# In the first expert layer a piece's second product runs three steps behind its first instead of two, with a third buffer for the high part

## The chip, the cores and the metric

The kernel runs on one NeuronCore of a Trainium2 chip. The metric is the device time of one execution in microseconds (us), median of three runs. Five engines work at once, each through its own queue in order: TensorE (PE, matrix products into PSUM), VectorE (DVE), ScalarE (ACT), GpSimd (POOL), and SyncE (SP), which here issues nearly all DMAs. PEld is TensorE's loading of weights, which overlaps the products.

## The reference, cut to what matters

```python
attn_out = _attn_ref(...)                 # linear attention, 8 x 8 heads, 576 tokens
x = attn_out ... reshape(B * S, H * D)    # 4608 tokens x 512
# first expert layer
h = x @ w_in                              # 512 -> 2048
g = h - np.tanh(h)
x = (g @ w_out).astype(np.float32)        # 2048 -> 512
# second expert layer
a = x @ w1
b = x @ w2
h = a * b @ w3
return (h @ w_out).astype(np.float32)
```

## The kernel before

Three stages follow one another: `attention()`, `moe1()` (the first expert layer) and `moe2()` (the second). Every fp32 operand of a large product is split into a high and a low part, so that one product is three TensorE products (high x high, low x high, high x low) summed in PSUM. In the names, `wih` and `wil` are the high and low part of a weight, `gh` and `gl` those of g.

**The first expert layer.** The 4608 tokens are 9 blocks of 512 (`NB`), the 2048 hidden columns 16 chunks of 128 (`NFC`). Step n = 16 j + i handles chunk i of block j, so there are 144 steps, numbered from 0. A step has two products on TensorE, of 12 matmuls of 128x512 each. The first, `mm1(n)` (L444, its matmuls are L456, tile `h`), gives a 128x512 tile of h. The second, `mm2` (L518, matmuls L527, tile `y`), multiplies g by 128 rows of `w_out` and adds into four banks y0 to y3 (`ps_y`, one buffer each), which gather a block over its 16 steps. Between the two lies `act_g(n)` (L470), which makes g = h - tanh(h), with a polynomial where h is small. It is a chain over three engines:

- ACT: u = h squared (L480), t = tanh h (L481), s (L482);
- DVE: p from h and u (L486), t = h - t (L488), p from s and p (L490), a mask into u (L492), a copy under that mask into t (L494);
- ACT: `gh`, the high part of t (L498); POOL: `gl` = t - `gh` (L499).

**What sets the order.** The schedule is by hand: every engine runs its instructions in the order in which the program writes them. The loop over n (L580) writes `mm1(n)`, then `mm2(n - LAG)` with `LAG = 2`, then `act_g(n)`. So TensorE's queue reads `mm1(n)`, `mm2(n-2)`, `mm1(n+1)`, `mm2(n-1)` and so on. Tiles `gh` and `gl` have two buffers each (`p3`), h three (`ps_h`).

**The end of a block.** Where `mm2` finishes a block, it hands the four y banks to the `act_g` of the same loop pass, as `ys`. There `y_out` (L504) copies them to SBUF: y0 to y2 on ACT behind s (L513), y3 on DVE behind the masked copy L494 (L515), and SP stores them (L516). The next block's first `mm2` writes the same banks, so it waits for these copies. With `LAG = 2` the block that ends at step 16j - 1 is copied in `act_g(16j + 1)`, and `mm2(16j)` comes in the pass behind.

**Work in between.** Into `act_g` and behind it the loop puts single operations on other things (`some()`, up to six): the conversion of 64-bit weights to high and low parts (`conv_steps`, L84: absolute value `et` on ACT L94, a maximum and a shift on DVE L98 and L101, a merge L104 on DVE, an integer part `ec` on ACT L109, an add on POOL L112, high part `wh` on ACT L116, low part `wl` on POOL L119), from step 0 to 13 for late chunks and from 16 to about 128 for the second layer's weights. Every third of the first twelve steps of a block ends with the split of a part of the next block's x (`split_x`: `xh` on ACT L747, `xl` on POOL L748).

**The seam to the second layer.** For n from 144 on, `mm3_half` takes the place of `mm1`: the first `LAG` tiles of the second layer's first product (tile `ab`) are made there, and `mm3` (L627) takes them and makes the others itself.

Of the kernel before, what the change touches and what calls it, by code (L numbers as in the profile page):

```python
# [9 lines left out]
F32R = mybir.dt.float32r  # L10
U32 = mybir.dt.uint32
# [33 lines left out]

TINY = 2.0 ** -15
FC_EARLY = 13


@with_exitstack  # L50
def kernel(ctx, tc, qk_in, v_in, w_phi, w_in, w_out, w12, w3t_in, wo2, out):
# [22 lines left out]
    def slot(kind, i, shape):  # L74
        pool = wpool if i < FC_EARLY else late[0]
        return tuple(pool.tile(shape, F32R, tag=f"{kind}{e}{i}", name=f"{kind}{e}{i}") for e in ("h", "l"))
# [3 lines left out]
    def words(raw, dt=U32):  # L80
        r = raw.bitcast(dt).rearrange("p (n two) -> p n two", two=2)
        return r[:, :, 0], r[:, :, 1]

    def conv_steps(pool, pre, n, load, dst, nb=1):  # L84

        o = {}

        def s_load():
            o["raw"] = pool.tile([128, n], I64, tag=f"{pre}raw", name=f"{pre}raw")
            load(o["raw"])  # L90

        def s_abs():
            o["t"] = pool.tile([128, n], U32, tag=f"{pre}t", name=f"{pre}t", bufs=nb)
            ACT.activation(o["t"].bitcast(F32), words(o["raw"], F32)[1], ACTF.Abs)  # L94

        def s_max():
            t = o["t"].bitcast(F32)
            DVE.tensor_scalar(t, t, TINY, None, ALU.max)  # L98

        def s_shift():  # L100
            DVE.tensor_scalar(o["t"], o["t"], 3, 0x3FFFFFF8, ALU.logical_shift_left, ALU.bitwise_and)  # L101

        def s_a():
            DVE.scalar_tensor_tensor(o["t"], words(o["raw"])[1], 0xC0000000, o["t"], ALU.bitwise_and, ALU.bitwise_or)  # L104

        def s_c():

            o["c"] = pool.tile([128, n], U32, tag=f"{pre}c", name=f"{pre}c", bufs=nb)
            ACT.activation(o["c"], words(o["raw"])[0], ACTF.Copy, scale=2.0 ** -29)  # L109

        def s_add():
            POOL.tensor_tensor(o["t"], o["t"], o["c"], ALU.add)  # L112

        def s_hi():
            o["hi"], o["lo"] = dst()
            ACT.activation(o["hi"], o["t"].bitcast(F32), ACTF.Copy)  # L116

        def s_lo():
            POOL.tensor_tensor(o["lo"], o["t"].bitcast(F32), o["hi"].bitcast(F32), ALU.subtract)  # L119

        return [s_load], [s_abs, s_max, s_shift], [s_c, s_a], [s_add], [s_hi], [s_lo]
# [15 lines left out]
    def w_out_chunk(pool, i, part=0, of=1, pre="c", nb=1):  # L137
        c = slice(part * DM // of, (part + 1) * DM // of)

        def dst():  # L140
            if part == 0:
                slots["out", i] = slot("wo", i, [128, DM])
            return tuple(t[:, c] for t in slots["out", i])

        return conv_steps(pool, pre, DM // of, lambda raw: SP.dma_start(raw, w_out[i * 128:(i + 1) * 128, c]), dst, nb)
# [3 lines left out]
    def attention():  # L149
        with ExitStack() as es:  # L150
# [215 lines left out]
            chunks = []  # L366
            for i in range(FC_EARLY):
                chunks += [w_in_chunk(pool, i), w_out_chunk(pool, i)]
# [92 lines left out]
    def moe1():  # L461
        with ExitStack() as es:
            p1 = es.enter_context(tc.tile_pool(name="m1", bufs=1))
            p2 = es.enter_context(tc.tile_pool(name="m2", bufs=2))
            p3 = es.enter_context(tc.tile_pool(name="m3", bufs=2))
            ps_y = es.enter_context(tc.tile_pool(name="ps_y", bufs=1, space=PSUM))

            gg, yy = {}, {}
# [1 line left out]
            def act_g(n, x, ys):  # L470
                def some():
                    if x:
                        x.pop(0)()

                h = hh[n]
                u = p2.tile([128, 512], F32, tag="u", name="u")
                s = p1.tile([128, 512], F32, tag="s", name="s")
                t = p2.tile([128, 512], F32, tag="t", name="t")
                p = p1.tile([128, 512], F32, tag="p", name="p")
                ACT.activation(u, h, ACTF.Square)  # L480
                ACT.activation(t, h, ACTF.Tanh)  # L481
                ACT.activation(s, u, ACTF.Square, bias=c1_sb)  # L482
                for d in range(3):
                    y_out(ys, d)
                some()
                DVE.scalar_tensor_tensor(p, h, C2, u, ALU.mult, ALU.mult)  # L486
                some()
                DVE.tensor_tensor(t, h, t, ALU.subtract)  # L488
                some()
                DVE.scalar_tensor_tensor(p, s, C0, p, ALU.add, ALU.mult)  # L490
                some()
                DVE.tensor_scalar(u, u, TLIM * TLIM, None, ALU.is_le)  # L492
                some()
                DVE.copy_predicated(t, u.bitcast(U32), p)  # L494
                some()
                gh = p3.tile([128, 512], F32R, tag="gh", name="gh")
                gl = p3.tile([128, 512], F32R, tag="gl", name="gl")
                ACT.activation(gh, t, ACTF.Copy)  # L498
                POOL.tensor_tensor(gl, t, gh.bitcast(F32), ALU.subtract)  # L499
                y_out(ys, 3)  # L500
                del hh[n]
                gg[n] = gh, gl
# [64 lines left out]
            late_chunks = []  # L567
            for i in range(FC_EARLY, NFC):
                for f in (w_in_chunk, w_out_chunk):
                    for part in range(2):  # L570
                        c = f(p2, i, part, 2, "e", 3)
# [4 lines left out]
            for i, f in enumerate(pending):  # L576
                place([[f]], 6 + 6 * i)
            n_all = NB * NFC
            LAG = 2
            for n in range(n_all + LAG):  # L580
                j, i = divmod(n, NFC)
                if n < n_all:
                    mm1(n)
                else:
                    mm3_half(n - n_all)
                ys = mm2(n - LAG) if n >= LAG else None
                if n >= n_all:
                    for d in range(4):
                        y_out(ys, d)
                if n >= n_all - 1 and n % 2:  # L590

                    i = (n - n_all + 1) // 2
                    t = [slot("wo", 12 + 2 * i + a, [128, DM]) for a in range(2)]
                    for e in range(2):
                        for a in range(2):
                            SP.dma_start(t[a][e].bitcast(F32), w3t_d[e][i][:, a * DM:(a + 1) * DM])
                    w3t[i] = [[t[j // 4][e][:, j % 4 * 128:(j % 4 + 1) * 128] for j in range(8)] for e in range(2)]
                if n < n_all:
                    x = list(extra.get(n, []))
                    act_g(n, x, ys)  # L600
                    for f in x:
                        f()
                    if i % 3 == 0 and i < 12:
                        xa = load_x(j + 1, i // 3) if j + 1 < NB else (load_y(0, i // 3), None)
                    if i % 3 == 1 and i < 12 and xa[1] is not None:
                        mul_x(*xa)
                    if i % 3 == 2 and i < 12:
                        split_x(j + 1, i // 3, xa[0])
                i = n - (n_all - NFC + 1)
                if 0 <= i < NFC:  # L610
                    slots["w12", i] = slot("wi", i, [128, NK, 128])
                    for e in range(2):
                        SP.dma_start(fc_view(slots["w12", i][e]).bitcast(F32), w12_d[e][i])
                i -= LAG
                if 0 <= i < 8:
                    slots["wo2", i] = slot("wo", i, [128, DM])
                    for e in range(2):
                        SP.dma_start(slots["wo2", i][e].bitcast(F32), wo2_d[e][i])


    def moe2():
        with ExitStack() as es:
# [4 lines left out]
            def mm3(j, i):  # L627
                pss = []
                for e in range(2):
                    n = 16 * j + 2 * i + e  # L630
                    if n > 1:
                        mm3_half(n)
                    ps = ab_ps.pop(n)
                    pss.append(ps)
                    if e == 0:
                        a = p2.tile([128, 512], F32, tag="a", name="a")
                        ACT.activation(a, ps, ACTF.Copy)
                t = p2.tile([128, 512], F32, tag="t", name="t")
                DVE.tensor_tensor(t, pss[1], a, ALU.mult)  # L639
                if i == 0:  # L640
                    hl = tuple(p2.tile([128, 512], F32R, tag=f"ab0{e}", name=f"ab0{e}") for e in ("h", "l"))
                else:
                    hl = slot("wo", i, [128, DM])
                ACT.activation(hl[0], t, ACTF.Copy)
                DVE.tensor_tensor(hl[1], t, hl[0].bitcast(F32), ALU.subtract)
                ab[j, i] = hl
# [158 lines left out]
```

## Time and profile before

| what | value |
|---|---|
| median of three runs | 1865.39 us (1864.75 to 1865.60) |
| the profiled execution | 1864.26 us, of which the span from the first to the last instruction is 1862.5 us |
| attention | from 0 to 389 us of the span |
| first expert layer | from 389 to 1231 us |
| second expert layer | from 1231 us to the end |
| busy: PE, DVE, ACT, POOL | 97%, 53%, 42%, 40% of the span |

Times are counted from the start of the span. A row of the timeline gives start, duration, engine, line, operation and tile, and in brackets how long the engine had been idle and what released it. Matmuls overlap and their ends are modelled, so an idle figure of PE is best checked by the distance between starts. A wait for several things is put down to the one that came last.

### The profile page before, as it was taken

The numbers are of one execution on the slowest core, as the hardware profiler recorded it, in microseconds if no ns is written. First come the engines' busy times: TensorE is split into PE (matmuls) and PEld (weight loads), VectorE is DVE, ScalarE is ACT, GpSimd is POOL, SyncE is SP. The second block draws the span as 40 slices with busy tenths as digits, with TensorE's granted clock in tenths as the row PEclk, the third lists the DMA queues.
The fourth block names the chain that finished last, engine by engine and source line by source line (L and its number), as shares of the span: only waits on it lengthen the run. The fifth ranks groups of instructions, "written<-read, shape, count | busy, mean of one in ns | idle before, by whom it ended". The sixth has DMA issues, their size and how long they took to land.

```text
span 1862.5 us, 27570 instructions
## 1 busy us (share of the span) xinstructions
PE 1797.4 (97%) x10176; PEld 1409.6 (76%) x10176; DVE 995.1 (53%) x1649; ACT 785.0 (42%) x1601; POOL 744.3 (40%) x750
## 2 busy tenths in 40 slices
PE   7999899999999999999999999999999999999999
PEld 5666666667777777777777777878888888888887
DVE  6777777847677777777777776521121112112111
ACT  4656566535555555545555555422122112112211
POOL 5767677725455655555555564300011001001100
PEclk9999999999999999999999999999999999999999
DMA  4444445422233333333333324552001101100100
GB/s 151 143 144 153 148 152 175 122 65 64 65 94 96 99 101 108 100 97 100 99 98 102 114 91 148 174 175 84 30 23 40 34 29 29 41 34 23 35 23 23
DMA packets 99944, 168.86 MB, mean 91 GB/s; under 512 B 13920, under 2 KB 46048, under 8 KB 99808
## 3 DMA queue, kind: packets, MB, share of 16 engines
q1 hardware_dynamic: 99648, 167.02, 28.6%
q8 instruction: 80, 1.31, 0.3%
q14 instruction: 56, 0.46, 0.1%
q10 hardware_dynamic: 160, 0.07, 0.0%
HBM read 117.46 MB, written 49.58 MB: 90 GB/s over the span
## 4 chain that ended last, share of the span: by engine, by line
PE 52%; DVE 22%; ACT 16%; issue 5%; DMA 3%; SPq 1%; ACTq 0%; DVEq 0%; POOL 0%
PE ab L456 21%; PE o L657 11%; DVE p L490 6%; DVE t L494 6%; ACT gh L498 4%; DVE u L492 4%; PE y L527 3%; ACT u L480 3%; PE p L188 3%; PE h L456 3%; ACT s L482 3%; PE o L319 3%; PE o L680 2%; PE kv L266 2%; DVE et L104 2%
## 5 line engine op out<-in xcount | busy, mean ns | idle before, releaser
L499 POOL TENSOR_TENSOR gl<-t,gh 128x512 fp32r<-128x512 f32 x144 | 186.6, 1296 | 287.6 <-ACT gh L498 202.9
L748 POOL TENSOR_TENSOR xl<-xn,xh 128x512 fp32r<-128x512 f32 x72 | 93.6, 1299 | 498.7 <-ACT xh L747 498.6
L498 ACT ACTIVATE gh<-t 128x512 fp32r<-128x512 f32 x144 | 91.0, 632 | 367.0 <-DVE t L494 338.9
L527 PE MATMUL y<-gl,woh 128*128 128x512 f32 x576 | 231.4, 402 | 13.9 <-POOL gl L499 12.8
L527 PE MATMUL y<-gh,woh 128*128 128x512 f32 x576 | 228.2, 396 | 14.6 <-DVE yo L515 7.1
L486 DVE SCALAR_TENSOR_TENSOR p<-h,u 128x512 f32<-128x512 f32 x144 | 99.6, 692 | 234.5 <-ACT t L481 234.5
L527 PE MATMUL y<-gh,wol 128*128 128x512 f32 x576 | 224.8, 390 | 0.0
L456 PE MATMUL h<-xh,wih 128*128 128x512 f32 x576 | 224.3, 389 | 0.0
L456 PE MATMUL h<-xh,wil 128*128 128x512 f32 x576 | 224.1, 389 | 0.0
L456 PE MATMUL h<-xl,wih 128*128 128x512 f32 x576 | 224.1, 389 | 0.0
L456 PE MATMUL ab<-xh,wih 128*128 128x512 f32 x576 | 224.1, 389 | 0.0
L456 PE MATMUL ab<-xh,wil 128*128 128x512 f32 x576 | 224.1, 389 | 0.0
L456 PE MATMUL ab<-xl,wih 128*128 128x512 f32 x576 | 224.1, 389 | 0.0
L639 DVE TENSOR_TENSOR t<-ab,a 128x512 f32<-128x512 f32 x72 | 49.8, 692 | 297.4 <-PE ab L456 294.4
L527 PEld LDWEIGHTS y<-gl,woh 128*128 128x128 f32 x576 | 108.0, 188 | 60.1 <-POOL gl L499 38.6
L527 PEld LDWEIGHTS y<-gh,woh 128*128 128x128 f32 x576 | 108.2, 188 | 45.1 <-DVE yo L515 10.1
L195 DVE TENSOR_REDUCE m<-p 128x4 f32<-128x512 f32 (+1 forms) x145 | 98.7, 681 | 80.4 <-PE p L188 80.0
L494 DVE COPY_PREDICATED t<-u,p 128x512 f32<-128x512 uint32 x144 | 127.4, 885 | 3.2
L208 ACT ACTIVATE kp<-dk 128x512 f32<-128x512 f32 x144 | 82.9, 626 | 109.6 <-DVE dk L197 75.3
L490 DVE SCALAR_TENSOR_TENSOR p<-s,p 128x512 f32<-128x512 f32 x144 | 128.2, 890 | 0.0
L456 PEld LDWEIGHTS h<-xh,wih 128*128 128x128 f32 x576 | 108.1, 188 | 22.8 <-issue 0.2
L456 PEld LDWEIGHTS h<-xh,wil 128*128 128x128 f32 x576 | 108.2, 188 | 22.6
(106 smaller groups left out, 3539.7 us busy)
## 6 DMA issues: line engine op xcount, KB each, us to landing
qk<-in_qk SPq DMA_DIRECT2D x33, 576.0 KB
v<-in_v SPq DMA_DIRECT2D x32, 320.0 KB
xn<-y_d SPq DMA_DIRECT2D x37, 256.0 KB
num_d<-st SPq DMA_DIRECT2D x128, 72.0 KB
xn<-num_d SPq DMA_DIRECT2D x36, 256.0 KB
out<-o SPq DMA_DIRECT2D x36, 256.0 KB
y_d<-yo SPq DMA_DIRECT2D x35, 256.0 KB
eraw<-in_w SPq DMA_DIRECT2D x32, 256.0 KB
```

The lines of the kernel that those rows point to most:

```text
L195: DVE.tensor_reduce(m[:, :n], what[g][:, j], AX.X, ALU.max, apply_absolute_value=True)
L208: ACT.activation(kp[g][:, sgn, span(js)], dk[g][:, span(js)], ACTF.Exp, scale=1.0 - 2 * sgn)
L456: PE.matmul(ps, a[:, kk, :], b[kk], start=m == 0, stop=m == 3 * NK - 1)
L486: DVE.scalar_tensor_tensor(p, h, C2, u, ALU.mult, ALU.mult)
L490: DVE.scalar_tensor_tensor(p, s, C0, p, ALU.add, ALU.mult)
L492: DVE.tensor_scalar(u, u, TLIM * TLIM, None, ALU.is_le)
L494: DVE.copy_predicated(t, u.bitcast(U32), p)
L498: ACT.activation(gh, t, ACTF.Copy)
L499: POOL.tensor_tensor(gl, t, gh.bitcast(F32), ALU.subtract)
L527: PE.matmul(yy[j][d], w[:, c], x, start=i == 0 and m == 0, stop=i == NFC - 1 and m == 2)
L657: PE.matmul(ps, a[:, c], w, start=m == 0, stop=m == 23)
L748: POOL.tensor_tensor(lo, a, hi.bitcast(F32), ALU.subtract)
```

## The change

`LAG` becomes 3 for the whole kernel: the loop writes `mm1(n)`, `mm2(n-3)`, `act_g(n)`. Pool `p3` gets three buffers, so `gh` has three; `gl` is held at two by its own argument. To make room, the conversion's tile `c` (at most three buffers before) has at most two. Since `LAG` is also the number of `ab` tiles made at the seam, `mm3` starts making its own at the fourth (L630), and the passes that load the transposed third weight move so that they stay behind the same `mm2`.

```diff
+LAG = 3
+
...
-            o["c"] = pool.tile([128, n], U32, tag=f"{pre}c", name=f"{pre}c", bufs=nb)
+            o["c"] = pool.tile([128, n], U32, tag=f"{pre}c", name=f"{pre}c", bufs=min(nb, 2))
...
-            p3 = es.enter_context(tc.tile_pool(name="m3", bufs=2))
+            p3 = es.enter_context(tc.tile_pool(name="m3", bufs=3))
...
                 gh = p3.tile([128, 512], F32R, tag="gh", name="gh")
-                gl = p3.tile([128, 512], F32R, tag="gl", name="gl")
+                gl = p3.tile([128, 512], F32R, tag="gl", name="gl", bufs=2)
...
             n_all = NB * NFC
-            LAG = 2
             for n in range(n_all + LAG):
...
-                if n >= n_all - 1 and n % 2:
-
-                    i = (n - n_all + 1) // 2
+                if n >= n_all and n % 2 == 0:
+
+                    i = (n - n_all) // 2
...
-                    if n > 1:
+                    if n >= LAG:
                         mm3_half(n)
```

The copies of a finished block move with `mm2`, by one step. On ACT's queue, about the last of these places (`act_g` of steps 129 and 130; `yo` are the copies of y0 to y2), the rows before are:

```order
L498 ACTIVATE gh<-t 128x512
L480 ACTIVATE u<-h 128x512
L481 ACTIVATE t<-h 128x512
L482 ACTIVATE s<-u,c_sb 128x512
L513 ACTIVATE yo<-y_11485 128x512
L513 ACTIVATE yo<-y_11486 128x512
L513 ACTIVATE yo<-y_11487 128x512
L498 ACTIVATE gh<-t 128x512
L480 ACTIVATE u<-h 128x512
L481 ACTIVATE t<-h 128x512
L482 ACTIVATE s<-u,c_sb 128x512
L498 ACTIVATE gh<-t 128x512
```

and with the change, at the same place on ACT:

```order
L500 ACTIVATE gh<-t 128x512
L482 ACTIVATE u<-h 128x512
L483 ACTIVATE t<-h 128x512
L484 ACTIVATE s<-u,c_sb 128x512
L500 ACTIVATE gh<-t 128x512
L482 ACTIVATE u<-h 128x512
L483 ACTIVATE t<-h 128x512
L484 ACTIVATE s<-u,c_sb 128x512
L515 ACTIVATE yo<-y_11528 128x512
L515 ACTIVATE yo<-y_11529 128x512
L515 ACTIVATE yo<-y_11530 128x512
L500 ACTIVATE gh<-t 128x512
```

The three copies stand behind the s of step 130, one whole step later than before.

On DVE's queue, about the first end of a block (steps 17 and 18; `et` are the maximum and the shift of a conversion, `yo` is the copy of y3), the rows before are:

```order
L494 COPY_PREDICATED t<-u,p 128x512
L515 COPY yo<-y_5211 128x512
L486 SCALAR_TENSOR_TENSOR p<-h,u 128x512
L98 TENSOR_SCALAR et<-et 128x256
L488 TENSOR_TENSOR t<-h,t 128x512
L101 TENSOR_SCALAR et<-et 128x256
L490 SCALAR_TENSOR_TENSOR p<-s,p 128x512
L492 TENSOR_SCALAR u<-u 128x512
L494 COPY_PREDICATED t<-u,p 128x512
```

and with the change:

```order
L496 COPY_PREDICATED t<-u,p 128x512
L488 SCALAR_TENSOR_TENSOR p<-h,u 128x512
L100 TENSOR_SCALAR et<-et 128x256
L490 TENSOR_TENSOR t<-h,t 128x512
L103 TENSOR_SCALAR et<-et 128x256
L492 SCALAR_TENSOR_TENSOR p<-s,p 128x512
L494 TENSOR_SCALAR u<-u 128x512
L496 COPY_PREDICATED t<-u,p 128x512
L517 COPY yo<-y_5258 128x512
```

The copy of y3 moves from the end of step 17 to the end of step 18; the rest of DVE's order is as it was.

## Rows read from the trace of the kernel before

**Rows 1.** The page, part 4: the chain that ended last, by engine.

```profile
PE 52%; DVE 22%; ACT 16%; issue 5%; DMA 3%; SPq 1%; ACTq 0%; DVEq 0%; POOL 0%
```

**Rows 2.** The waits: engine, line, releaser; us in total, times, longest.

```profile
ACT gh L498 <- DVE t L494: 338.9, 134, 4.0
DVE p L486 <- ACT t L481: 234.5, 144, 5.6
ACT gh L498 <- PE y L527: 22.6, 8, 3.2
ACT u L480 <- PE h L456: 4.2, 8, 0.6
```

**Rows 3.** Line L527, the second product: what its idle PE and PEld waited for.

```profile
  POOL gl L499: 51.4, 86
  DVE yo L515: 17.2, 14
  ACT yo L513: 13.9, 14
```

**Rows 4.** The timeline, ACT: the tile `gh` of steps 2 and 132.

```profile
410.39 0.63 ACT L498 ACTIVATE gh<-t 128x512 fp32r<-128x512 f32 x1 [1.41 <-DVE t L494]
...
1162.73 0.63 ACT L498 ACTIVATE gh<-t 128x512 fp32r<-128x512 f32 x1 [2.55 <-DVE t L494]
```

**Rows 5.** The timeline, PE: two first products in a stretch without waits.

```profile
1171.48 0.39 PE L456 MATMUL h<-xh,wih 128*128 128x512 f32 x1
...
1176.92 0.39 PE L456 MATMUL h<-xh,wih 128*128 128x512 f32 x1
```

**Rows 6.** The timeline, all engines, at the last end of a block (steps 129 and 130).

```profile
1144.70 0.72 ACT L482 ACTIVATE s<-u,c_sb 128x512 f32<-128x512 f32 x1
...
1147.10 0.76 DVE L494 COPY_PREDICATED t<-u,p 128x512 f32<-128x512 uint32 x1
...
1148.16 0.69 DVE L515 COPY yo<-y 128x512 f32<-128x512 f32 x1 [0.30 <-DMA y_d<-yo]
...
1148.72 1.29 POOL L499 TENSOR_TENSOR gl<-t,gh 128x512 fp32r<-128x512 f32 x1 [3.50 <-issue]
...
1149.45 0.73 ACT L482 ACTIVATE s<-u,c_sb 128x512 f32<-128x512 f32 x1
...
1149.70 0.39 PE L456 MATMUL h<-xh,wih 128*128 128x512 f32 x1
```

**Rows 7.** The timeline, ACT and DVE, at two block ends (steps 33 and 18).

```profile
588.73 1.57 ACT L513 ACTIVATE yo<-y 128x512 f32<-128x512 f32 x3
590.47 0.45 ACT L94 ACTIVATE et<-eraw 128x256 f32<-128x256 f32 x1
...
590.95 0.62 DVE L98 TENSOR_SCALAR et<-et 128x256 f32<-128x256 f32 x1 [0.47 <-ACT et L94]
...
501.13 0.90 DVE L98 TENSOR_SCALAR et<-et 128x256 f32<-128x256 f32 x1 [0.24 <-ACT et L94]
```

**Rows 8.** The timeline, DVE and POOL: L490 alone, and beside a POOL instruction.

```profile
589.46 0.68 DVE L490 SCALAR_TENSOR_TENSOR p<-s,p 128x512 f32<-128x512 f32 x1
...
601.57 1.20 DVE L490 SCALAR_TENSOR_TENSOR p<-s,p 128x512 f32<-128x512 f32 x1
...
601.48 0.73 POOL L119 TENSOR_TENSOR wl<-et,wh 128x256 fp32r<-128x256 f32 x1
```

**Rows 9.** The timeline, ACT and DVE: a `gh` put down to PE (step 35).

```profile
604.74 0.63 ACT L498 ACTIVATE gh<-t 128x512 fp32r<-128x512 f32 x1 [2.85 <-PE y L527]
...
603.47 1.17 DVE L494 COPY_PREDICATED t<-u,p 128x512 f32<-128x512 uint32 x1
```

**Rows 10.** Attention: a PE gap, and windows (us, engines' busy time, granted clock, DMA).

```profile
26.64 0.44 PE L301 MATMUL kv<-ident,kvs 128*128 128x128 f32 x2 [1.58 <-DVE kvs L296]
...
20.00:30.00 10.00, 7.54 (x62) 5.77 (x62) 8.59 (x13) 6.00 (x13) 8.47 (x10) 0.87 0.44 144
30.00:40.00 10.00, 10.00 (x95) 5.98 (x93) 6.46 (x12) 5.43 (x11) 7.49 (x10) 0.79 0.36 108
```

## The prediction, made before the changed kernel was timed

> **What bounds the kernel now.** Only the first expert layer changes its order, so I look for what sets its pace. The page's chain of waits comes first: it runs through PE for only 52% of the span, and through DVE and ACT for 22% and 16%, although PE is busy nearly all the time [rows 1]. PE's own idle time says where PE gives way: before the second product it waited 51.4 us in 86 places for `gl`, and 31 us at block ends for the copies of the y banks [rows 3]. That looks like a lack of lead, which a third step of lag would cure. It isn't, and the list of waits shows why: ACT waits for DVE at `gh` in 134 of 144 steps, DVE waits for ACT at p in all 144, and ACT waits for PE at u in only 8 steps, 4.2 us together [rows 2]. ACT and DVE play ping-pong. ACT makes `gh` only when DVE's masked copy of the step is done, and only behind `gh` come u and t of the next step in ACT's queue; DVE can't begin that step before t. Neither waits for PE, since h has long been there.
>
> The pace of this ping-pong: `gh` of step 2 starts at 410.39 and of step 132 at 1162.73 [rows 4], 130 steps in 752.3 us, 5.79 us a step. PE needs 5.44 us for a step's two products (24 matmuls) where nothing holds it [rows 5], so one product is 2.72 us. The elementwise loop is slower by 0.35 us a step, 5.6 us over a block of 16. PE has to lose these 5.6 us per block somewhere. It loses them now at `gl` and at the block ends. More lag can move that loss, but can't remove it while the loop doesn't wait for PE.
>
> One line of the waits seems to say that it does: `gh` put down to PE, 8 times, 22.6 us [rows 2]. One of the eight is step 35: of ACT's 2.85 us idle, DVE's copy took all but the last 0.1 (it ended at 603.47 + 1.17 = 604.64, `gh` started at 604.74) [rows 9]. The rest of the 22.6 us belongs to DVE, and the third `gh` buffer frees about nothing.
>
> **Part 1, the waits for `gl`: gain 0 on the path.** With three steps of lag `gl` is a step older when PE wants it, so nearly all of the 86 waits go. What is late next is the end of the block. The first product of a new block writes the y banks; the copies that free them stand in `act_g` behind the s of step 16j + 2, where they stood behind that of step 16j + 1. PE, now ahead by up to a step more, arrives there and waits for what the ping-pong has left over: up to 5.6 us per block in one place, where it was about 2.
>
> **Part 2, the last block end: 2.0 us later.** Behind it there are no conversions left, the loop is quicker than PE, and PE runs without waits to the end of the kernel, so this end of a block sets the end. It comes one elementwise step later: s of step 130 starts at 1149.45, that of 129 at 1144.70 [rows 6], 4.75 us. When PE goes on there, it has one first product more behind it than before, worth 2.72 us. 4.75 - 2.72 = 2.03 us later, for an unchanged elementwise loop. The same holds at each earlier block end, but there the loop goes on regardless and nothing is passed on.
>
> **Part 3, the copies move in ACT's and DVE's order: 0, between -0.9 and +1.6 us.** Three copies block ACT for 1.57 us [rows 7], now one step later. Whoever queues behind them matters only where DVE waits for it. At step 33 it did: the conversion's absolute value came behind the copies, and DVE's maximum waited 0.47 us for it [rows 7]. The same order of conversion work stands at one more block end, so taking the copies away there gives at most 2 x 0.47 = 0.9 us. At step 18, where they now stand, the maximum comes right behind p in DVE's queue and already waited 0.24 us for the absolute value [rows 7]; 1.57 us more ahead of that costs at most 1.57. In between its own duration, 0.90 us here beside a POOL instruction and 0.62 at step 33 [rows 7], gives something back. I take gain and loss as equal; they have nearly the same size. The copy of y3 on DVE lies beside ACT's `gh`, u and t, as it did, and costs nothing; if that cover went, 0.69 us per block [rows 6].
>
> **Part 4, `gl` now waits for PE: 2.8 us, between 0 and 5.5.** `gl` keeps two buffers, so `gl` of step 16j + 2 needs `mm2(16j)` to be done, and that product now waits for the copy of y3 of the same step 16j + 2. From the start of that copy to the end of the product it took 1148.16 to 1149.70, 1.54 us [rows 6]; the copy starts about 0.1 us behind DVE's masked copy where no DMA holds it. `gl` used to start 0.86 us behind the masked copy (1147.10 + 0.76 to 1148.72) [rows 6]. So POOL is held for 1.54 + 0.1 - 0.86 = 0.78 us, once per block. Queued behind it on POOL are the split `xl` of the next block's x and the conversion's low part and add. PE doesn't need this `gl` soon, but DVE and POOL get in each other's way: p at L490 takes 0.68 us alone and 1.20 us where POOL's 0.73 us `wl` started just ahead of it [rows 8]. Shifted POOL work thus falls on L490 and what follows it. The trace has no step with that shift. Below, POOL's idle time takes it up and it costs 0; above, DVE loses the whole 0.78 us at each of the 7 block ends that conversions follow, 5.5 us. I take about half, 0.4 us per block end (nearest to the 0.52 us that L490 lost), 7 x 0.4 = 2.8.
>
> The rule for this is in the Trainium skill, SBUF — State Buffer, section SBUF: two separate sides: POOL and a DVE instruction with two SBUF inputs share one pair of ports, which the first holds for its whole instruction while the other waits. That agrees with L490's 1.20 us. Taken strictly, every shifted POOL instruction that starts ahead of a DVE one would cost its whole remaining time, which leads to the upper end, and 2.7 us more than my sum.
>
> **Parts at nothing.** The conversion's `c` with two buffers: a buffer is filled and added within one step, and there is less than one conversion a step, so the third was never waited for; if it were, it would be ACT's 0.45 us for such a tile [rows 7] now and then. The seam: `ab` 2 is made one place earlier and PE's work stays the same; the loads of the third weight keep their place behind the same second product. SP gets the stores of a block one step later, behind other loads that have two steps to spare.
>
> **The sum.** 2.0 + 0 + 2.8 = 4.8 us. The profiled execution took 1864.26 us (span 1862.5), so 1869.1; the median of the runs shown is 1.1 us above it, and from it I say 1865.4 + 4.8 = 1870.2 us.
>
> **The rivals.**
>
> (a) *The ping-pong does wait for PE, and gets faster.* Then the loop would run at PE's 5.44 us and the 51.4 us of waits for `gl` would leave the path: 1865.4 - 130 x 0.35 = 1820 us. It decides as soon as u or `gh` start late because of PE by 0.35 us in the average step. For it speaks the size of the waits in rows 3; against it the 4.2 us in 8 steps of rows 2 and the 0.1 us of rows 9. A small gain, by a luckier order of the copies and no price in part 4, is likelier: -1 to -4 us. Both together 0.07.
>
> (b) *Nothing is left of part 4, and part 3 gains.* 2.0 - 0.9 + 0 = +1.1, 1866.5 us. For it: POOL is busy for 40% of the span only. Against: the shift falls in the step with `xl`, POOL's fullest. 0.20.
>
> (c) *TensorE's clock falls.* In attention, behind a PE gap of 1.58 us with short matmuls around it [rows 10], the granted clock was at half (1.2 GHz) for 0.13 x 2 x 10 + 0.21 x 2 x 10 = 6.8 us of the two windows. PE's waits at the block ends, up to 5.6 us where they were about 2, are longer than that gap. Half a clock for 6.8 us costs PE 3.4 us. In the inner blocks the 5.6 us of slack covers this, with longer holds of `gl`; at the last block end it is on the path: 1870.2 + 3.4 = 1873.6 us. Against: a fall at the block end before eats the slack, and then PE's wait at the last one is short. 0.15. The Trainium skill, TensorE: Matmul & The Clock Gate, section Why this matters for your kernels, says the same as advice, to leave no idle gaps between bursts of matmuls; whether gaps of this size among dense matmuls suffice, no row of before shows.
>
> **How the numbers follow.** The forecast, later by 1.5 to 7 us, has 0.58, (b) 0.20, (c) 0.15, (a) 0.07. A measurement of this kernel can tell 0.2% (3.7 us) from no change. Of the forecast's 0.58 I put 0.36 above that line and 0.22 below, since 4.8 lies just over it; of (c) 0.14 above. So slower 0.50, same 0.22 + 0.20 + 0.01 = 0.43, faster 0.07. The range goes from just under (b) to the forecast with part 4 in full and the last loss of (c) or part 3: 2.0 + 1.6 + 5.5 = 9.1, so 1865.0 to 1874.5.
>
> **What would show it.** Of after: the waits of L529 for `gl` shrink to a few us, while the waits for `yo` grow from 31 to more than 60; `gh` to `gh` still takes 5.8 us a step; ACT's u still doesn't wait for PE; POOL's `gl` waits for PE once per block, some 0.8 us; the last block's first `mm2` starts about 4.7 us later, and the second layer some 2 to 7 us later. I am wrong if the step from `gh` to `gh` falls towards 5.44 us, or if the second layer starts earlier than at 1231 us.

## The result, and the profile after

The changed kernel took 1875.4 us (median of four runs, 1873.9 to 1879.1) beside 1865.1 us (four runs, 1863.6 to 1865.6): a ratio of 1.0060, 95% interval 1.0042 to 1.0077. It is 10.3 us slower, where 4.8 us was forecast, and it lies just outside the range (1865.0 to 1874.5). The profiled execution took 1875.86 us, its span 1874.1 (before 1862.5).

What the page's chain by engine and the list of waits (us in total, times, longest) say after:

```profile
PE 60%; DVE 18%; ACT 14%; issue 5%; DMA 3%; SPq 1%; POOL 0%; DVEq 0%; ACTq 0%
...
ACT gh L500 <- DVE t L496: 365.2, 137, 5.7
DVE p L488 <- ACT t L483: 229.0, 143, 5.6
POOL gl L501 <- PE y L529: 55.9, 15, 4.6
PE y L529 <- ACT yo L515: 34.2, 8, 5.0
```

and what the idle time of the second product's line, PE and PEld together, waited for:

```profile
  ACT yo L515: 71.8, 16
  POOL gl L501: 15.5, 21
  DVE yo L517: 6.3, 7
```

Beside [rows 1 to 3]: the waits for `gl` fell from 51.4 to 15.5 us, those for the copies `yo` grew from 31 to 78, and ACT and DVE still wait for each other in nearly every step. What is new is the line of POOL's `gl` waiting for PE. Not all of its 55.9 us is lost time, as POOL often has nothing else to do.

The pace of the elementwise loop, by the `gh` of steps 2 and 132, as in [rows 4]:

```profile
410.20 0.63 ACT L500 ACTIVATE gh<-t 128x512 fp32r<-128x512 f32 x1 [1.35 <-DVE t L496]
...
1173.68 0.63 ACT L500 ACTIVATE gh<-t 128x512 fp32r<-128x512 f32 x1 [2.53 <-DVE t L496]
```

130 steps took 763.5 us where they took 752.3. Most steps take what they took before, to 0.02 us, and single steps that differ by up to 1.5 us either way cancel to -0.1 us up to step 128. What is left sits in the step behind each block end. Step 16j + 3 (19, 35, and so on to 115) is longer than before by 0.46, 2.82, 1.44, 0.94, 1.50, 1.08 and 1.39 us, 9.6 together. In the step ahead of it `gl` started 0.97, 3.19, 1.76, 1.14, 1.86, 1.25 and 1.80 us later behind `gh` than it does elsewhere.

The last block end, in the timeline of all engines, as in [rows 6]:

```profile
1159.37 1.57 ACT L515 ACTIVATE yo<-y 128x512 f32<-128x512 f32 x3
...
1160.01 0.70 PE L529 MATMUL y<-gh,woh 128*128 128x512 f32 x1 [3.89 <-ACT yo L515]
...
1161.16 0.74 DVE L496 COPY_PREDICATED t<-u,p 128x512 f32<-128x512 uint32 x1
1161.37 0.63 PE L529 MATMUL y<-gh,woh 128*128 128x512 f32 x1
...
1161.79 0.63 PE L529 MATMUL y<-gh,wol 128*128 128x512 f32 x1
...
1162.12 0.69 DVE L517 COPY yo<-y 128x512 f32<-128x512 f32 x1 [0.23 <-DMA y_d<-yo]
...
1163.76 0.39 PE L529 MATMUL y<-gh,woh 128*128 128x512 f32 x1
...
1163.99 0.39 PE L529 MATMUL y<-gh,wol 128*128 128x512 f32 x1
...
1164.45 0.39 PE L458 MATMUL h<-xh,wih 128*128 128x512 f32 x1
...
1164.79 1.29 POOL L501 TENSOR_TENSOR gl<-t,gh 128x512 fp32r<-128x512 f32 x1 [5.50 <-DMA y_d<-yo]
```

PE stood idle for about 4 us before this product. Its matmuls then follow each other at 0.42 us (1161.37 to 1161.79), and only at its end at 0.23 again (1163.76 to 1163.99). The granted clock is at its lower level here, 1.2 GHz in place of 2.4: so it was for a time at all eight block ends, where before it was at none, and its mean over the span fell from 0.998 to 0.988. The product ends at 1164.45, 14.75 us after the 1149.70 of [rows 6], with one first product (2.72 us) less to do behind it: 12.0 us later. 9.3 of these come from the steps before, 2.7 from this block end.

### The profile page after: what moved, and what is told of

Its sections match the earlier page's. It is cut to its first block, busy times and chain, and to the rows that moved or that the text cites. A ratio compares the mean times of both kernels' runs of the same rounds, so it can differ in the third digit from the quotient of the medians.

```text
span 1874.1 us, 27564 instructions
## 1 busy us (share of the span) xinstructions
PE 1794.7 (96%) x10176; PEld 1423.9 (76%) x10176; DVE 1009.0 (54%) x1649; ACT 783.5 (42%) x1601; POOL 746.5 (40%) x750
## 4 chain that ended last, share of the span: by engine, by line
PE 60%; DVE 18%; ACT 14%; issue 5%; DMA 3%; SPq 1%; POOL 0%; DVEq 0%; ACTq 0%
PE ab L458 21%; PE o L658 10%; PE y L529 7%; PE h L458 6%; DVE p L492 5%; DVE t L496 5%; PE p L190 3%; ACT gh L500 3%; PE o L321 3%; DVE u L494 3%; ACT u L482 3%; ACT s L484 2%; PE o L681 2%; PE kv L268 2%; PE o L330 2%
## 5 line engine op out<-in xcount | busy, mean ns | idle before, releaser
L529 PE MATMUL y<-gh,woh 128*128 128x512 f32 x576 | 233.0, 405 | 36.8 <-ACT yo L515 34.2
L529 PE MATMUL y<-gh,wol 128*128 128x512 f32 x576 | 230.3, 400 | 0.0
L529 PEld LDWEIGHTS y<-gl,woh 128*128 128x128 f32 x576 | 111.8, 194 | 34.1 <-POOL gl L501 10.5
L492 DVE SCALAR_TENSOR_TENSOR p<-s,p 128x512 f32<-128x512 f32 x144 | 134.9, 937 | 0.0
L529 PEld LDWEIGHTS y<-gh,wol 128*128 128x128 f32 x576 | 112.0, 194 | 22.9
```

Source lines behind the costliest of these rows:

```text
L529: PE.matmul(yy[j][d], w[:, c], x, start=i == 0 and m == 0, stop=i == NFC - 1 and m == 2)
```

## Experiments

The kernels ran in two sets of four, each beside runs of the kernel before (median 1864.2 us in the first set, 1863.5 in the second, and 1865.1 beside the changed kernel). So a time set against the changed kernel's 1875.4 is uncertain by 1 to 2 us; "slower by" or "faster by" means against the kernel before of the same set. T1 is the theory that the place of the copies costs, by the held `gl` and by the last block end.

**Keep TensorE busy at the block ends.**

```diff
+                if i == 0 and j > 0:
+                    for _ in range(16):
+                        w = ps_w.tile([128, 512], F32, tag="w", name="w")
+                        PE.matmul(w, wh[:, :128], gh, start=True, stop=True)
```

> The changed kernel, and ahead of the first second product of each of blocks 1 to 7 (mm2(16j)) sixteen further matmuls of the same size into a spare PSUM bank, whose results are not used; they fill the 3.6 to 5.2 us in which TensorE stands idle there. T1 (at a block end TensorE's idle time brings its clock down to half, so mm2(16j) takes 4.3 to 6.5 us, gl of step 16j+2 is held for 1.7 us on average in place of the 0.78 us forecast, and some 85% of it is passed on): mm2(16j) falls back to some 3.5 us, the hold to 0.3 to 0.6 us, and seven block ends give back about 7 x 0.85 x 1.25 = 7.4 us, the last one 0.65 us more: 1867.3 us (1866 to 1870). Rival C0 (the clock has no share in it; the time goes by the place of the copies, the buffers or the order of transfers alone): 1875.4 us (1874 to 1877).

It took 1887.8 us, slower by 23.6 and more than either theory said. The filling was too long: in the timeline of PE, at block 4,

```profile
781.35 8.75 PE L530 MATMUL w<-gh,woh 128*128 128x512 f32 x16
789.93 0.40 PE L534 MATMUL y<-gh,woh 128*128 128x512 f32 x1
```

sixteen matmuls took 8.75 us, 0.55 each, since each one waits for the matmul before it to end. So `mm2(16j)` came later still, at full clock, and the run became a larger dose of the hold: `gl` held for 3.1 to 4.4 us in place of 1.0 to 3.2, and the elementwise loop 20.0 us longer up to step 128 in place of 9.5. It says nothing yet on the clock.

**The copies back in their place, the lag of three kept.**

```diff
-                if n >= n_all:
+                if n > n_all:
...
-                if n < n_all:
-                    x = list(extra.get(n, []))
-                    act_g(n, x, ys)
+                m = n - 1
+                j, i = divmod(m, NFC)
+                if 0 <= m < n_all:
+                    x = list(extra.get(m, []))
+                    act_g(m, x, ys)
```

> The changed kernel with the lag of three on TensorE and the third buffer as they are, but with the elementwise part of step n written behind mm1(n+1) and mm2(n-2), so that the copies of a block's last banks stand in step 16j+1 of ScalarE and VectorE, as in the kernel before, and not in step 16j+2. T1 (the place of the copies makes the cost: by them mm2(16j) comes late, holds gl of step 16j+2, and the last block end grows; the lag itself costs nothing and takes one first product, 2.72 us, off the end): 1865.1 - 2.7 = 1862.4 us (1861.5 to 1864.0), no wait of GpSimd for TensorE at gl, full clock at the block ends. Rival B0 (the lag, the third buffer of gh or the second-only buffer of c cost by themselves, whatever the place of the copies): 1868 us or more.

It took 1858.9 us, ratio to before 0.9970 (0.9958 to 0.9983): the loss is gone, and a gain of 5.4 us stands in its place, 2.6 us below T1's range. In PE's timeline at the last block end

```profile
1142.83 0.50 PE L529 MATMUL y<-gh,woh 128*128 128x512 f32 x1 [0.47 <-ACT yo L515]
...
1146.51 0.40 PE L458 MATMUL h<-xh,wih 128*128 128x512 f32 x1
```

`mm2(128)` starts after half a microsecond of idle time and ends 3.2 us earlier than before (1146.51 against 1149.70), with 2.7 us less to do behind it. The 3.2 come from attention, which ended 3.6 us earlier in this profile though its code is the same (last section); the steps between are 0.5 us longer. That the lag takes work off the end shows in what follows this product: to the end of the span it is 710.6 us here and 709.6 to 710.6 in all eight kernels with the lag of three, but 712.8 in the kernel before and 712.7 with the buffers alone. That the rest of the gain is attention's rests on this one profile. B0 falls.

**The buffers alone, lag of two.**

```diff
-            o["c"] = pool.tile([128, n], U32, tag=f"{pre}c", name=f"{pre}c", bufs=nb)
+            o["c"] = pool.tile([128, n], U32, tag=f"{pre}c", name=f"{pre}c", bufs=min(nb, 2))
...
-            p3 = es.enter_context(tc.tile_pool(name="m3", bufs=2))
+            p3 = es.enter_context(tc.tile_pool(name="m3", bufs=3))
...
-                gl = p3.tile([128, 512], F32R, tag="gl", name="gl")
+                gl = p3.tile([128, 512], F32R, tag="gl", name="gl", bufs=2)
```

> The kernel before, lag of two, with only the buffers of the change: three for gh, two for gl, at most two for the word c of the weights' split. T1 (the buffers by themselves cost nothing): 1865.1 us (1864.4 to 1865.8). Rival B1 (c with two buffers makes ScalarE wait for GpSimd, or the moved addresses cost): a part of the 10.3 us, 1867 us or more.

It took 1856.9 us, ratio 0.9952 (0.9937 to 0.9967), faster by 7.4 us, which neither theory had. The timeline of ACT and DVE, `gh` of steps 2 and 132 and one masked copy with the `gh` behind it:

```profile
409.78 0.63 ACT L498 ACTIVATE gh<-t 128x512 fp32r<-128x512 f32 x1 [1.36 <-DVE t L494]
...
1155.68 0.63 ACT L498 ACTIVATE gh<-t 128x512 fp32r<-128x512 f32 x1 [2.47 <-DVE t L494]
...
464.90 1.18 DVE L494 COPY_PREDICATED t<-u,p 128x512 f32<-128x512 uint32 x1
...
466.12 0.63 ACT L498 ACTIVATE gh<-t 128x512 fp32r<-128x512 f32 x1 [1.35 <-DVE t L494]
```

130 steps take 745.9 us in place of 752.3: nearly every step is some 0.06 us shorter, and four are about 0.5 longer. `gh` starts 0.04 us behind the masked copy (466.08 to 466.12), where before it was 0.10 [rows 9]. By the order of instructions nothing differs but a wait of ACT:

```
L498 ACTIVATE gh<-t 128x512 [waits DVE_49,PE_49]
L498 ACTIVATE gh<-t 128x512 [waits DVE_49]
L500 ACTIVATE gh<-t 128x512 [waits DVE_49,PE_49]
```

(before, with the buffers alone, and in the changed kernel). The trace has the second wait as an instruction of its own on ACT, an event semaphore of 0.02 us: before, one stands just ahead of `gh` in 141 of 144 steps, and there `gh` starts 0.09 us behind the masked copy (median). In the other three steps, and in all 144 with the buffers alone, there is none, and `gh` starts 0.03 us behind it.

With two buffers `gh(n)` needs `mm2(n-2)`, which stands behind `mm1(n)` in PE's order; with three it needs `mm2(n-3)`, which stands ahead of `mm1(n)`, and u of the same step has already waited for that. With the lag of three, three buffers need `mm2(n-3)` too, and that now stands behind `mm1(n)`: the second wait is back. T2 is the theory that this second wait costs about 0.06 us a step although it has long been satisfied.

**The held `gl` in another buffer.**

```diff
+                if n % NFC == 2 and n > NFC:
+                    gl = p1.tile([128, 512], F32, tag="yo", name="gy", bufs=3).bitcast(F32R)
+                else:
+                    gl = p3.tile([128, 512], F32R, tag="gl", name="gl", bufs=2)
```

> The changed kernel, but gl of step 16j+2 (blocks 1 to 7) is written into the next of the three yo buffers in place of the next of the two gl buffers, so that it need not wait for mm2(16j). Copies, lag and order stay, and so does the idle time of TensorE with the halved clock. T1 (the late mm2(16j) costs by the held gl alone): the waits of GpSimd for TensorE at gl go, the seven extra periods of step 16j+3 (9.6 us in all) fall to 0 to 0.3 us each, and the end of the last block still costs 2.7 us: 1875.4 - 9.6 + 1 = 1866.8 us (1865 to 1869). Rival P0 (the moved copies themselves, or GpSimd's instructions beside VectorE's, make the longer steps, and the wait at gl is covered): 1872 us or more.

It took 1869.5 us, 5.9 less than the changed kernel and 0.5 above T1's range (slower by 5.3, where the change was slower by 10.3). Six of the seven extra periods fell to 0.0 (-0.08 to 0.02 us). In block 2 the tile waited for a store of `yo` instead, and steps 35 to 38 lost 4.7 us. For six block ends T1 holds, and P0 falls; the seventh spoils the sum, so the run with a buffer of its own below was made.

**Lag of three, four buffers for `gh`.**

```diff
-                u = p2.tile([128, 512], F32, tag="u", name="u")
+                u = p2.tile([128, 512], F32, tag="u", name="u", bufs=1)
...
-                gh = p3.tile([128, 512], F32R, tag="gh", name="gh")
+                gh = p3.tile([128, 512], F32R, tag="gh", name="gh", bufs=4)
```

> The changed kernel with four buffers for gh in place of three (one of u makes room). Lag, copies and order stay; the only thing that goes from the loop is the second wait of ScalarE's gh: by the order of instructions, gh of before and of after waits for VectorE's t and for a second product that is long done (PE), in the buffers-only kernel and here for VectorE alone. T2 (a second wait costs ScalarE 0.06 us at each gh even where it is satisfied, as the buffers-only kernel showed: gh began 0.03 us after the copy that it waits for in place of 0.09, and a step was 0.06 us shorter): 0.06 x 110 = 6.6 us: 1875.4 - 6.6 = 1868.8 us (1867 to 1871), the held gl at the block ends as in the changed kernel. Rival B2 (the buffers-only kernel gained by something that goes with the lag of two): 1875.4 us (1874 to 1877).

It took 1867.8 us, 7.6 less than the changed kernel. Part of that is the set: slower by 4.2 in place of 10.3, it gained 6.1 us, and 130 steps took 757.4 us in place of 763.5. T2 holds and B2 falls: four buffers need `mm2(n-4)`, ahead of `mm1(n)`, and the second wait is gone with the lag of three as well.

**Both: copies in their place, four buffers for `gh`.** The edit that puts the copies back and the one just above, together.

> The kernel with the lag of three and the copies back in step 16j+1, and with four buffers for gh (one of u makes room), so that gh waits for VectorE alone. T1 with T2 (the lag takes a first product off the end, the copies' place keeps gl free, the second wait costs 0.06 us a step, and the three add up): 1858.9 - 6.6 = 1852.3 us (1850 to 1854.5), faster than the buffers-only kernel at 1856.9. Rival E0 (the two gains are the same one, or another row takes the place of the wait): 1856 us or more.

It took 1853.4 us, ratio 0.9945 (0.9932 to 0.9957): about 10 us faster than the kernel before, where the change was 10 slower. The gains add up to within about 1 us of what T1 and T2 said, or 2 us if each is taken against its own set, and E0 falls. It is the lowest median of all, though the 1856.9 of the buffers alone has an interval that overlaps.

**The filling in the right size.** The sixteen matmuls become one group of fourteen. The edit fills the end of block 8 as well as those of blocks 1 to 7 that the expectation names:

```diff
-                    for _ in range(16):
-                        w = ps_w.tile([128, 512], F32, tag="w", name="w")
-                        PE.matmul(w, wh[:, :128], gh, start=True, stop=True)
+                    w = ps_w.tile([128, 512], F32, tag="w", name="w")
+                    for k in range(14):
+                        PE.matmul(w, wh[:, :128], gh, start=k == 0, stop=k == 13)
```

> The changed kernel, and ahead of mm2(16j) of blocks 1 to 7 fourteen further matmuls of the same size that add up in one spare PSUM bank, whose result is not used. In the run before (sixteen matmuls, each started and ended by itself) each of them took 0.547 us in place of 0.227, so that they held mm2(16j) up by 8.7 us, longer than the idle time that they were to fill; in one group fourteen should take 3.2 us. T1 (the halved clock makes the hold longer): clock full at the block ends, mm2(16j) some 3.5 us, hold 0.3 to 0.8 us: 1867.5 us (1865.5 to 1870.5). Rival C0 (the clock has no share): 1875.4 us (1874 to 1877).

It took 1875.3 us, what C0 expected. Windows of 10 us around the ends of blocks 4 and 5 (the columns end with the granted clock, the DMA share and GB/s), first of the changed kernel:

```profile
782.00:792.00 10.00, 7.29 (x25) 5.78 (x26) 6.68 (x11) 7.65 (x16) 6.16 (x6) 0.83 0.46 159
878.00:888.00 10.00, 9.43 (x31) 7.56 (x32) 8.69 (x14) 5.53 (x13) 5.85 (x6) 0.72 0.49 157
```

and of the kernel with the fourteen matmuls:

```profile
782.00:792.00 10.00, 7.07 (x30) 5.18 (x29) 6.56 (x13) 6.87 (x14) 5.03 (x5) 1.00 0.45 158
878.00:888.00 10.00, 6.96 (x30) 5.13 (x29) 7.43 (x12) 7.31 (x16) 6.26 (x6) 1.00 0.46 158
```

Here the clock stayed up (at block ends 3 to 8; at the first two it still fell). Yet at those six `gl` was still held, by 0.9 to 1.3 us, 1.15 on average, where the changed kernel has 1.65. The extra periods sum to 5.7 us in place of 8.0. The gain sits at block ends 3, 5, 7 and 8, where in the changed kernel `mm2(16j)` ended 2.2 to 2.4 us behind the start of y3's copy and here 1.5; at 4 and 6 it ended 1.5 us behind it in both, and the hold is the same (1.14 and 1.15, 1.25 and 1.23 us). So by these profiles the clock makes the smaller part: 2.4 us in six block ends. That this doesn't show in the time is due to the first two block ends, which cost 5.9 us here and 3.3 in the changed kernel; whether that is chance stays open.

**A third buffer for `gl`.**

```diff
-                u = p2.tile([128, 512], F32, tag="u", name="u")
+                u = p2.tile([128, 512], F32, tag="u", name="u", bufs=1)
...
-                gl = p3.tile([128, 512], F32R, tag="gl", name="gl", bufs=2)
+                gl = p3.tile([128, 512], F32R, tag="gl", name="gl")
```

> The changed kernel with three buffers for gl (one of u makes room), so that gl of step 16j+2 need not wait for mm2(16j) at any block end; copies, lag, order and gh's second wait stay. In the run with gl in a yo buffer the extra periods of step 16j+3 went to 0.0 at six of seven block ends, but two gl of block 2 waited for stores of yo instead and 4.7 us came in at steps 35 to 38. T1: the seven extra periods go (9.6 us), the end of the last block (2.7 us) and the copies ahead of step 18's absolute value (0.8 us) stay: 1875.4 - 9.6 = 1865.8 us (1864 to 1868). Rival P1 (the 2.8 us of block 2 come by the late copies and the transfer ahead of them, not by the held gl): 1868.5 us or more.

It took 1865.6 us where T1 said 1865.8, 9.8 less than the changed kernel. That it is so close is partly luck, since the kernel before was 1.6 us faster in this set: against it the run is slower by 2.0 (ratio 1.0011, 1.0002 to 1.0019), so 8.3 of the 10.3 us are gone. In the trace the seven extra periods fell from 9.6 to 0.5 us. What stays is in block 2 (0.6 us at step 35, 0.4 at step 36), where the copy of y3 comes late here too. P1 falls. The list of waits

```profile
POOL gl L501 <- ACT gh L500: 273.8, 139, 24.4
PE y L529 <- ACT yo L515: 23.9, 8, 4.0
```

has no `gl` that waits for PE, while PE still waits for the copies at all eight block ends. At seven of the eight the clock still falls, and it costs little, because no one waits for PE.

## Why the prediction was half right

**What bounds the kernel, and Part 1: right.** The loop of ACT and DVE sets the pace and doesn't wait for PE: with the third step of lag the waits for `gl` fell from 51.4 to 15.5 us and nothing was gained by it. Rival (a) as written didn't come.

**Part 2: right in kind, 0.7 us short.** 2.7 us in place of 2.03. The rest is the last `mm2(16j)` at half clock, 4.44 us (1160.01 to 1164.45) in place of 3.74 before. With the clock up it took 3.7 (the fourteen matmuls).

**Part 3: right in sum, partly by luck.** Step 18 lost 0.81 us (bound 1.57); the steps that the copies left gave back 0.5 to 0.6 us at three block ends in place of two. Steps 24, 101 and 123 lost 0.5 us each, for which the prediction had no term; they do so with the buffers alone, too. All but the held `gl` sums to about -0.1 us, forecast 0.

**Part 4: the step that failed.** Mechanism and place were right, the size was not: 9.6 us in place of 2.8, and above the 5.5 given as its upper bound. Two factors failed.

- The hold, 0.78 us. Its term of 1.54 us, from the start of y3's copy to the first matmul behind the product, was right: at block end 4 of the changed kernel it is the same (DVE, PE and POOL).

```profile
787.63 0.68 DVE L517 COPY yo<-y 128x512 f32<-128x512 f32 x1
...
789.17 0.40 PE L458 MATMUL h<-xh,wih 128*128 128x512 f32 x1
...
789.48 1.30 POOL L501 TENSOR_TENSOR gl<-t,gh 128x512 fp32r<-128x512 f32 x1 [2.74 <-PE y L529]
```

But the sum took that matmul for the moment at which `gl` can start, and POOL starts it 0.31 us later. With the 0.80 us by which `gl` usually follows the masked copy, in place of 0.86, this makes 0.1 + 1.54 + 0.31 - 0.80 = 1.15 us, the average that was measured with the clock up. Three of the seven holds are longer by the clock: at block ends 3, 5 and 7 the product's matmuls are at the lower level to its end (0.43 us apart), and the 1.54 us become 2.2 to 2.4. The seven average 1.7. In block 2 the hold is 3.2: there the copy of y3 itself waits for a store of the buffer that it writes, as the rows of the changed kernel on DVE, POOL and SP's queue show,

```profile
601.00 0.69 DVE L517 COPY yo<-y 128x512 f32<-128x512 f32 x1 [1.95 <-DMA y_d<-yo]
...
603.01 1.72 DVE L492 SCALAR_TENSOR_TENSOR p<-s,p 128x512 f32<-128x512 f32 x1
...
602.88 1.29 POOL L501 TENSOR_TENSOR gl<-t,gh 128x512 fp32r<-128x512 f32 x1 [4.61 <-PE y L529]
604.14 1.74 POOL L749 TENSOR_TENSOR xl<-xn,xh 128x512 fp32r<-128x512 f32 x1
...
597.29 0.33 SPq L557 DMA_DIRECT2D eraw<-in_w  x1
597.67 1.44 SPq L518 DMA_DIRECT2D y_d<-yo  x3
```

The stores now stand behind a load (`eraw`) on SP's queue and left at 597.67, though the third copy was done at 596.93; this is the move that the prediction had costed at nothing.

- The part passed on: forecast a half, measured 0.8 (9.6 of 12.0 us). Step 67 shows how. In the changed kernel, DVE and POOL:

```profile
790.99 1.32 DVE L106 SCALAR_TENSOR_TENSOR et<-eraw,et 128x256 uint32<-128x256 uint32 x1
...
790.74 1.29 POOL L749 TENSOR_TENSOR xl<-xn,xh 128x512 fp32r<-128x512 f32 x1
```

and with three buffers for `gl`, the same two:

```profile
787.58 0.42 DVE L106 SCALAR_TENSOR_TENSOR et<-eraw,et 128x256 uint32<-128x256 uint32 x1
...
786.17 1.31 POOL L749 TENSOR_TENSOR xl<-xn,xh 128x512 fp32r<-128x512 f32 x1
```

Undisturbed, `gl` and `xl` fall into the time in which DVE waits for ACT's t. Held by 1.14 us, `xl` falls on DVE's merge, which takes 1.32 us in place of 0.42: 0.90 of the 0.94 us that the step lost. The strict reading of the Trainium skill, SBUF — State Buffer, section SBUF: two separate sides, which the prediction set aside, is the one that this row bears out: the merge ended only behind `xl`, at 792.31 against 792.03.

**Rival (c): its clock came, its price not.** The granted clock fell at all eight block ends, not at one, and 0.15 was too little. At the last one it cost 0.7 us and not 3.4. The sentence that the slack covers the inner blocks was wrong, since a longer hold of `gl` goes past PE's slack straight to DVE. By the profile with the fourteen matmuls the clock's part is 2.4 us in six block ends.

**"The third `gh` buffer frees about nothing": wrong for the buffer, right for the change.** [rows 9] had the price in it: the 0.1 us between DVE's copy and `gh` was taken as a remainder of one step, and it stands in nearly every step. With the lag of two the third buffer is worth 6.4 us by the trace and 7.4 by the medians; the lag of three uses it up.

So the loss of 10.3 us consists of 9.6 us in the steps behind the block ends, nearly all by the held `gl`, and 2.7 by the last block end; the rest of the trace gives about 0.7 back in the profiled execution, and the medians differ by a further 1.3.

## What to carry to other kernels

Where work is moved to a later step, look at each buffer that is freed by what is moved: here the copies of y freed PE, PE freed `gl`, and `gl` was on the path of the elementwise loop, since a POOL instruction that starts late makes DVE's beside it longer. Size such a hold up to the start of the instruction that is held, not to the end of the work that it waits for, and add what the change does to the clock and to the order of the transfers. And on a chain of engines that answer each other, count the waits of each instruction: one more buffer is worth having if it only turns a wait that is always satisfied into none.

## What the runs showed of the hardware

- A second wait, long satisfied, delayed ACT's `gh` by some 0.06 us at nearly every step: it starts 0.09 us behind the masked copy with it and 0.03 without (medians), and 130 steps take 752.3 us with it and 745.9 without.
- POOL's `gl` started 0.31 to 0.34 us behind the first matmul that follows the product it waits for, at seven of eight block ends (0.60 at the other).
- Idle gaps of 3.6 to 5.2 us among dense matmuls were followed each time, at eight of eight block ends, by the lower clock (0.42 us from matmul to matmul in place of 0.23). The Trainium skill, TensorE: Matmul & The Clock Gate, section Why this matters for your kernels, advises against such gaps; the prediction had no row to show that gaps of this size suffice, and now these do.
- Matmuls that each open and close a sum in the same bank, with a wait for the one before, took 0.55 us each (16 in 8.75 us), fourteen in one group 0.24 (3.33 us).
- Attention, the same code in every kernel here, ended up to 3.6 us apart. In four profiles (the copies in their place is one) the first `gh` started 3.4 to 3.6 us earlier than before; none of these four has a lowered clock between 180 and 220 us, where all the others but before itself do (0.96 to 0.98), and before has one at 30 us [rows 10]. Three of the four have a shorter one there. How often each happens wasn't measured, so the steps of single profiles were compared from step 2 on. The windows of the changed kernel and of the one with the copies in their place:

```profile
180.00:220.00 40.00, 35.76 (x394) 24.10 (x398) 30.34 (x50) 21.79 (x46) 27.52 (x34) 0.98 0.46 136
```

```profile
180.00:220.00 40.00, 37.07 (x424) 25.48 (x426) 29.89 (x51) 23.25 (x49) 27.89 (x34) 1.00 0.46 136
```
